# Feed-forward stage: the second products of a chunk's last two feature tiles as one block, token tile by token tile

## The chip, the core and the metric

The kernel runs on one core of a Trainium2 chip, as one program. The metric is the device time of one execution in microseconds (us). Before the change the median of three runs is 1665.53 us, the lowest 1661.75 and the highest 1668.51. Lower is better.

## What is computed

An attention with pooled queries (8 batches, 8 heads, 576 pooled query rows against 1152 keys, head size 64) is followed by a feed-forward part on its 4608 rows of 512 features. The change touches the feed-forward part alone:

```python
q_pool = q.reshape(B, H, S // factor, factor, D).mean(axis=3)
attn = softmax(scale * q_pool @ k^T);  x = (attn @ v), heads side by side   # 4608 x 512
h = x @ w_in            # 512 -> 2048
g = h - np.tanh(h)
out = g @ w_out         # 2048 -> 512
```

(The softmax line is the reference's five lines in short.)

## The kernel before

The attention fills the first half of the span and writes its result to `x_dram`; nothing of it changes. The feed-forward part then goes over the 4608 tokens in chunks: eight of 512 tokens and two of 256. Within a chunk it goes over 16 feature tiles of 128 hidden features, `fc` = 0 to 15 (`NF` = 16). Every fp32 operand is split into a high and a low part, so each product is three matmuls.

For one feature tile there are two blocks of work on TensorE (PE):

- the first product, in `hidden`: 12 matmuls into one buffer `ps_h` (three such PSUM buffers). We call it H(fc).
- the second product, in `second`: for each of the chunk's four token tiles of 128 tokens three matmuls that add `g_hi` and `g_lo` times `wo[fc]` into that token tile's sum. The sums lie in `ps_o`, four PSUM buffers, one for each token tile, and stay open over all 16 feature tiles. We call it S(fc): 12 matmuls.

Between the two, `hidden` makes g = h - tanh(h) from `ps_h`: six ScalarE (ACT) instructions (`g_u`, `g_t`, two `g_s`, `g_m` at lines 509 to 513, and `g_hi` at 520), six VectorE (DVE) ones (514 to 519) and `g_lo` on GpSimd (POOL). As this takes a while, a second product is made three feature tiles late: `waiting` holds what is still to be done, and after each H the oldest entry is taken once more than `LAG` = 3 are waiting (six in chunks of 256 tokens). A tick below marks the next chunk, so at a chunk's end PE's order is H15, S12, H0', S13, H1', S14, H2', S15, H3', S0'.

When S15 is done, `store` copies the four sums out of `ps_o` with four ACT instructions (line 539, into `o_s`, which has two buffers) and SP's queue sends each to `out`. S0' writes the same four `ps_o` buffers, so each token tile of S0' has to wait for its copy.

What sets the order: on PE, POOL and SP the instructions stand in the order of the code (`keep_in_program_order`). ACT and DVE are ordered by the tile framework's scheduler, which works from a timeline of its own at build time. Each engine then executes its list strictly in that order. The next chunk's rows of x are fetched by SP's queue at `fc` = 0, 3, 6 and 9 and divided and split on POOL up to `fc` = 12; `reciprocals` and the weight loads take place in the first chunk only.

The profile gives line 37 (the recording helper) to all PE, POOL and SP instructions; names of tiles tell them apart: `ps_h` is a first product, `ps_o` a second one, `o_s` a copy of a sum. `ps_o<-w` (a weight tile loaded ahead, `w`) marks S0 and S1, `ps_o<-wo` the others; `ps_h<-x,w` marks H0 to H3.

Of the kernel before, what the change touches and what calls it, by code (L numbers as in the profile page):

```python
# [8 lines left out]
F32 = mybir.dt.float32  # L9
# [34 lines left out]
def kernel(  # L44
# [18 lines left out]
    P = 128  # L63
    B, NP, _, _, SQ = q.shape
# [4 lines left out]
    DM, DFF = w_in.shape  # L69
    w_in, w_out = w_in.bitcast(I32), w_out.bitcast(I32)  # L70
    NF = DFF // P
# [22 lines left out]
    def load_x(tiles, raw, sp, mul, hi, t0, n):  # L94

        x_h, x_l = (t.rearrange("p (c n) -> p c n", c=NP) for t in tiles())

        t = {}

        def fetch(hp):  # L100
            x, r = t[hp] = raw(hp)
            sp.dma_start(x[:, 0:n], x_dram[hp, :, t0:t0 + n])
            c = t0
            while c < t0 + n:
                b, c1 = divmod(c, SQ)
                m = min(SQ - c1, t0 + n - c)
                for h in range(2):
                    sp.dma_start(r[h * 64:h * 64 + 64, c - t0:c - t0 + m],
                                 r_dram[b, hp, h:h + 1, c1:c1 + m].broadcast_to([64, m]))
                c += m  # L110

        def divide(hp):
            x, r = t[hp]
            mul.tensor_tensor(x[:, 0:n], x[:, 0:n], r[:, 0:n], op=ALU.mult)

        def hi_part(hp):
            hi(x_h[:, hp, 0:n], t[hp][0][:, 0:n])

        def lo_part(hp):
            mul.tensor_tensor(x_l[:, hp, 0:n], t[hp][0][:, 0:n], x_h[:, hp, 0:n].bitcast(F32), op=ALU.subtract)  # L120
        return x_h, x_l, [[lambda hp=hp, f=f: f(hp) for f in (fetch, divide, hi_part, lo_part)] for hp in range(NP)]
# [6 lines left out]
    def x_tile(i):  # L128
        return xp[i].tile([P, NP * 512], F32R, name="x")
# [5 lines left out]
    t, n = chunks.pop()  # L135
# [4 lines left out]
    with ExitStack() as actx:  # L140
# [10 lines left out]
        pe, act, dve, pool, sp = (InOrder(tc, e) for e in (nc.tensor, nc.scalar, nc.vector, nc.gpsimd, nc.sync))  # L151
# [185 lines left out]
        def reciprocals(eng, b, t):  # L337

            eng.tensor_scalar(t, t, 1e-9, None, op0=ALU.add)
            eng.reciprocal(t, t)  # L340

        def spread(dma, b, t):
            dma.dma_start(by_rows(r_dram[b]), t)
# [66 lines left out]
        wi, wo = [], []  # L410
# [39 lines left out]
        for u in range(end + 60):  # L450
            run(u, first)
            run(u, early)
            n, r = divmod(u, G)
# [19 lines left out]
    ps_o = ctx.enter_context(tc.tile_pool(name="ps_o", bufs=4, space=PSUM))  # L473

    pe, pool, sp = (InOrder(tc, e) for e in (nc.tensor, nc.gpsimd, nc.sync))
    halves = {}

    def weights(f1):
        while max(len(wi), len(wo)) < f1 or len(wo) < len(wi):
            f = len(wo)  # L480
            if f == len(wi):
                wi.append(wt.tile([P, 2, NP, P], F32R, name=f"wi{f}"))
                sp.dma_start(wi[f].bitcast(F32), wi_dram[f])
            if f >= len(wo):
                wo.append(wt.tile([P, 2, DM], F32R, name=f"wo{f}"))
                sp.dma_start(wo[f].bitcast(F32), wo_dram[f])
# [34 lines left out]
        pool.tensor_tensor(g_l, s1, g_h.bitcast(F32), op=ALU.subtract)  # L521
        return g_h, g_l, last

    def second(po, g_h, g_l, _, nt, fc):
        for j in range(nt):
            ts = slice(j * P, (j + 1) * P)
            for i, (g, w) in enumerate(((g_h, 0), (g_h, 1), (g_l, 0))):
                pe.matmul(po[j], g[:, ts], wo[fc][:, w],
                                 start=(fc == 0 and i == 0), stop=(fc == NF - 1 and i == 2))

    def store(po, t0, nt, ci):
        if ci == len(chunks) - 1:
            o_n = x_tile((ci + 1) % 2).bitcast(F32).rearrange("p (j n) -> p j n", n=DM)
        for j in range(nt):
            if ci == len(chunks) - 1:
                o_s = o_n[:, j]
            else:
                o_s = gp.tile([P, DM], F32, name="o_s", bufs=2)
            nc.scalar.activation(o_s, po[j], AF.Copy)  # L539
            sp.dma_start(out[t0 + j * P:t0 + (j + 1) * P, :], o_s)  # L540

    waiting = []
    xs = x0
    for ci, (t0, n) in enumerate(chunks):
        x_h, x_l, _ = xs
        po = []
        for fc in range(NF):
            if ci == 0:
                weights(min(NF, 5 + 2 * fc))

            load = []
            if ci + 1 < len(chunks):
                if fc == 0:
                    xs = load_x(lambda: (x_tile((ci + 1) % 2), x_tile((ci + 1) % 2)), x_raw, sp, pool,
                                lambda o, x: pool.tensor_scalar(o, x, 1.0, 0.0, op0=ALU.mult, op1=ALU.add), *chunks[ci + 1])
                load = [xs[2][(fc - x) // 3][i] for i, x in ((3, 3), (0, 0), (1, 2), (2, 2)) if (fc - x) % 3 == 0 and 0 <= fc - x < 3 * NP]
            for f in load:
                f()
            g = hidden(x_h, x_l, n, fc)
            if tot and fc == 3:  # L560
                with tc.issue_after(g[2]):
                    reciprocals(nc.vector, *tot[0])
                spread(sp, *tot.pop(0))

            def rest(po=po, g=g, fc=fc, t0=t0, nt=n // P, ci=ci):
                if fc == 0:
                    po += [ps_o.tile([P, DM], F32, name="ps_o") for _ in range(nt)]
                second(po, *g, nt, fc)
                if fc == NF - 1:
                    store(po, t0, nt, ci)  # L570
            waiting.append(rest)
            while len(waiting) > (LAG if n > 256 else 2 * LAG):
                waiting.pop(0)()
    while waiting:
        waiting.pop(0)()


_OUTS = [((4608, 512), 'float32')]
# [31 lines left out]
```

## Time and profile before

| | before |
|---|---|
| median of 3 runs, us | 1665.53 (1661.75 to 1668.51) |
| the profiled execution's own time, us | 1668.33 |
| its span, first to last instruction, us | 1666.5 |
| mean granted TensorE clock | 0.994 of full |
| PE busy in the span | 1621.7 us, 97% |
| DVE, ACT, POOL busy | 79%, 61%, 56% |

The feed-forward part takes the span from about 850 us to its end. In the profile a number in square brackets is idle time of the engine before an instruction, with what ended it. A row of the chain of waits is a piece of the path that ended last: its start, its length, and the work. A row of the view by stretches gives the stretch, its length, the busy time of PE with the count of its instructions, the granted clock (1.00 is full), the share of the DMA engines and GB/s.

### The profile page before, as it was taken

The numbers are of one execution on the slowest core, as the hardware profiler recorded it, in microseconds if no ns is written. First come the engines' busy times: TensorE is split into PE (matmuls) and PEld (weight loads), VectorE is DVE, ScalarE is ACT, GpSimd is POOL, SyncE is SP. The second block draws the span as 40 slices with busy tenths as digits, with TensorE's granted clock in tenths as the row PEclk, the third lists the DMA queues.
The fourth block names the chain that finished last, engine by engine and source line by source line (L and its number), as shares of the span: only waits on it lengthen the run. The fifth ranks groups of instructions, "written<-read, shape, count | busy, mean of one in ns | idle before, by whom it ended". The sixth has DMA issues, their size and how long they took to land.

```text
span 1666.5 us, 32223 instructions
## 1 busy us (share of the span) xinstructions
PE 1621.7 (97%) x12576; PEld 1251.9 (75%) x12576; DVE 1322.2 (79%) x1725; ACT 1021.2 (61%) x1865; POOL 939.8 (56%) x694
## 2 busy tenths in 40 slices
PE   5999999999999999999999999999999999999999
PEld 3666776777777677777778787887878787878897
DVE  7888889889888889888657677676767676776886
ACT  2655655656656556556566666566666666665776
POOL 2777878778778778778844243334334332422332
PEclk9999999999999999999999999999999999999999
DMA  3343443443344334335464101101010111010000
GB/s 139 118 136 107 139 136 108 126 134 122 124 128 130 124 115 144 123 106 163 143 242 158 38 26 40 37 14 51 26 51 26 38 39 38 26 37 15 25 27 26
DMA packets 72665, 147.86 MB, mean 89 GB/s; under 512 B 11136, under 2 KB 36672, under 8 KB 72512
## 3 DMA queue, kind: packets, MB, share of 16 engines
q1 hardware_dynamic: 72512, 145.80, 26.8%
q8 instruction: 99, 1.62, 0.4%
q14 instruction: 54, 0.44, 0.1%
HBM read 109.49 MB, written 36.27 MB: 87 GB/s over the span
## 4 chain that ended last, share of the span: by engine, by line
PE 84%; DVE 13%; ACT 2%; issue 1%; DMA 0%; DVEq 0%; ACTq 0%
PE ps L37 37%; PE ps_h L37 24%; PE ps_o L37 23%; DVE w L37 6%; DVE mx L37 6%; DVE nm L37 0%; DVE lo L37 0%; ACT g_s L512 0%; ACT g_m L513 0%; ACT g_s L511 0%; ACT g_u L509 0%; DMA q_n<-in_q_dram 0%; ACT g_hi L520 0%; ACT o_s L539 0%; ACT g_t L510 0%
## 5 line engine op out<-in xcount | busy, mean ns | idle before, releaser
L37 DVE TENSOR_REDUCE mx<-ps 128x2 f32<-128x768 f32 x480 | 434.3, 950 | 74.8 <-PE ps L37 74.7
L37 POOL TENSOR_TENSOR g_lo<-g_s,g_hi 128x512 fp32r<-128x512 f32 (+1 forms) x160 | 189.9, 1187 | 511.5 <-ACT g_hi L520 464.9
L37 ACT ACTIVATE p_f<-ps 128x576 f32<-128x576 f32 x576 | 361.5, 650 | 94.3 <-PE ps L37 79.7
L37 POOL TENSOR_TENSOR z<-p_f 128x576 f32<-128x576 f32 x192 | 279.6, 1456 | 154.7 <-ACT p_f L37 154.7
L37 PE MATMUL ps<-hi 64*128 64x288 f32 (+1 forms) x2112 | 316.9, 352 | 23.7 <-DVE mx L37 13.7
L37 PE MATMUL ps_h<-x,wi 128*128 128x512 f32 (+1 forms) x1440 | 327.2, 377 | 0.0
L37 PE MATMUL ps_o<-wo,g_hi 128*128 128x512 f32 x1008 | 311.6, 390 | 0.0
L37 PEld LDWEIGHTS ps_h<-x,wi 128*128 128x128 f32 x1440 | 260.0, 193 | 53.1
L37 PE MATMUL ps<-p_f,v 128*64 128x288 f32 x2304 | 293.5, 409 | 0.0
L37 PEld LDWEIGHTS ps<-hi 64*128 64x128 f32 x2112 | 194.6, 187 | 89.2 <-DVE mx L37 34.6
L509 ACT ACTIVATE g_u<-ps_h 128x512 f32<-128x512 f32 (+1 forms) x160 | 88.8, 555 | 267.8 <-PE ps_h L37 267.5
L37 PEld LDWEIGHTS ps<-p_f,v 128*64 128x64 f32 x2304 | 159.7, 137 | 113.7 <-ACT p_f L37 12.0
L514 DVE SCALAR_TENSOR_TENSOR ps_w<-g_u,ps_h 128x512 f32<-128x512 f32 (+1 forms) x160 | 102.9, 643 | 178.7 <-ACT g_t L510 177.0
L37 PEld LDWEIGHTS ps_o<-wo,g_hi 128*128 128x128 f32 x1008 | 187.5, 188 | 39.1
L37 POOL TENSOR_TENSOR z<-z,p_f 128x576 f32<-128x576 f32 x128 | 194.0, 1516 | 11.9 <-ACT p_f L37 2.0
L37 PE MATMUL ps_o<-wo,g_lo 128*128 128x512 f32 x504 | 196.3, 389 | 0.0
L37 PE MATMUL ps<-lo,hi 64*128 64x288 f32 x1152 | 171.0, 293 | 0.0
L37 PE MATMUL ps<-hi,lo 64*128 64x288 f32 x1152 | 170.9, 293 | 0.0
L37 PE MATMUL ps<-mb,ones_k 64*128 64x288 f32 x1152 | 170.3, 292 | 0.0
L37 ACT ACTIVATE o_s<-ps 128x288 f32<-128x288 f32 x64 | 26.3, 411 | 230.3 <-PE ps L37 230.3
L519 DVE COPY_PREDICATED g_s<-g_m,g_t 128x512 f32<-128x512 int32 (+1 forms) x160 | 116.2, 726 | 17.1 <-DVE g_s L518 0.9
L517 DVE SCALAR_TENSOR_TENSOR ps_w<-g_s,ps_w 128x512 f32<-128x512 f32 (+1 forms) x160 | 102.9, 643 | 16.6 <-ACT g_m L513 0.5
(68 smaller groups left out, 2398.9 us busy)
## 6 DMA issues: line engine op xcount, KB each, us to landing
q_n<-in_q_dram SPq DMA_DIRECT2D x32, 576.0 KB
kq<-in_k_dram SPq DMA_DIRECT2D x32, 576.0 KB
v<-in_v_dram SPq DMA_DIRECT2D x32, 576.0 KB
x_dram<-o_s SPq DMA_DIRECT2D x32, 288.0 KB
out_dram<-o_s SPq DMA_DIRECT2D x34, 256.0 KB
w_raw<-in_moe_w_in_dram SPq DMA_DIRECT2D x16, 512.0 KB
wi_dram<-w_hl SPq DMA_DIRECT2D x16, 512.0 KB
w_raw<-in_moe_w_out_dram SPq DMA_DIRECT2D x16, 512.0 KB
```

The costliest lines, as they stand in the source:

```text
L37: ins = self.tc.keep_in_program_order(f(*args, **kwargs))
L509: nc.scalar.activation(u, h, AF.Square)
L514: nc.vector.scalar_tensor_tensor(w, u, -P0, h, op0=ALU.add, op1=ALU.mult)
L517: nc.vector.scalar_tensor_tensor(w, s2, P2, w, op0=ALU.add, op1=ALU.mult)
L519: last = nc.vector.copy_predicated(s1, m.bitcast(I32), th).ins
```

## The change

`rest` is no longer a closure that makes one S; it takes an entry from `waiting`, and when that entry is feature tile 14 (`NF - 2`) it takes the one for 15 as well and makes both: for each token tile the three matmuls of 14 and then the three of 15. `store` follows at once. Nothing is added or left out; the same matmuls, copies and transfers are issued.

```diff
-    def second(po, g_h, g_l, _, nt, fc):
+    def second(po, j, g_h, g_l, fc):
+        ts = slice(j * P, (j + 1) * P)
+        for i, (g, w) in enumerate(((g_h, 0), (g_h, 1), (g_l, 0))):
+            pe.matmul(po[j], g[:, ts], wo[fc][:, w], start=(fc == 0 and i == 0), stop=(fc == NF - 1 and i == 2))
+
+    def rest():
+        po, nt, t0, ci, *x = waiting.pop(0)
+        x = [x]
+        if x[0][-1] == 0:
+            po += [ps_o.tile([P, DM], F32, name="ps_o") for _ in range(nt)]
+        if x[0][-1] == NF - 2:
+            x.append(waiting.pop(0)[4:])
         for j in range(nt):
-            ts = slice(j * P, (j + 1) * P)
-            for i, (g, w) in enumerate(((g_h, 0), (g_h, 1), (g_l, 0))):
-                pe.matmul(po[j], g[:, ts], wo[fc][:, w],
-                                 start=(fc == 0 and i == 0), stop=(fc == NF - 1 and i == 2))
+            for g in x:
+                second(po, j, *g)
+        if len(x) == 2:
+            store(po, t0, nt, ci)
...
-            def rest(po=po, g=g, fc=fc, t0=t0, nt=n // P, ci=ci):
-                if fc == 0:
-                    po += [ps_o.tile([P, DM], F32, name="ps_o") for _ in range(nt)]
-                second(po, *g, nt, fc)
-                if fc == NF - 1:
-                    store(po, t0, nt, ci)
-            waiting.append(rest)
+            waiting.append((po, n // P, t0, ci, *g[:2], fc))
             while len(waiting) > (LAG if n > 256 else 2 * LAG):
-                waiting.pop(0)()
+                rest()
     while waiting:
-        waiting.pop(0)()
+        rest()
```

On PE, at the first chunk's end, the order before is: the end of S14, then H2' (`ps_h_13198`), then S15 (`wo15`) over its four token tiles (`ps_o_12484` to `ps_o_12487`).

```order
L37 MATMUL ps_o_12487<-wo14_12560,g_lo_13023 128x512
L37 MATMUL ps_h_13198<-x_12302,w02_126 128x512 x4
L37 MATMUL ps_h_13198<-x_12303,w02_126 128x512 x4
L37 MATMUL ps_h_13198<-x_12302,w02_126 128x512 x4
L37 MATMUL ps_o_12484<-wo15_12612,g_hi_13068 128x512 x2
L37 MATMUL ps_o_12484<-wo15_12612,g_lo_13069 128x512
L37 MATMUL ps_o_12485<-wo15_12612,g_hi_13068 128x512 x2
L37 MATMUL ps_o_12485<-wo15_12612,g_lo_13069 128x512
L37 MATMUL ps_o_12486<-wo15_12612,g_hi_13068 128x512 x2
L37 MATMUL ps_o_12486<-wo15_12612,g_lo_13069 128x512
L37 MATMUL ps_o_12487<-wo15_12612,g_hi_13068 128x512 x2
L37 MATMUL ps_o_12487<-wo15_12612,g_lo_13069 128x512
```

In the order after, S14 (`wo14`) and S15 alternate by token tile ahead of H2' (here `ps_h_13222`). These rows are the last token tile of that block, then H2', H3' (`ps_h_13264`) and the start of S0' (`w03`).

```order
L37 MATMUL ps_o_12487<-wo14_12560,g_hi_13022 128x512 x2
L37 MATMUL ps_o_12487<-wo14_12560,g_lo_13023 128x512
L37 MATMUL ps_o_12487<-wo15_12612,g_hi_13068 128x512 x2
L37 MATMUL ps_o_12487<-wo15_12612,g_lo_13069 128x512
L37 MATMUL ps_h_13222<-x_12302,w02_126 128x512 x4
L37 MATMUL ps_h_13222<-x_12303,w02_126 128x512 x4
L37 MATMUL ps_h_13222<-x_12302,w02_126 128x512 x4
L37 MATMUL ps_h_13264<-x_12302,w04_128 128x512 x4
L37 MATMUL ps_h_13264<-x_12303,w04_128 128x512 x4
L37 MATMUL ps_h_13264<-x_12302,w04_128 128x512 x4
L37 MATMUL ps_o_13298<-w03_127,g_hi_13123 128x512 x2
L37 MATMUL ps_o_13298<-w03_127,g_lo_13124 128x512
```

So PE's order becomes H15, S12, H0', S13, H1', then S14 and S15 together, H2', H3', S0': S15 has moved ahead of H2', and two first products now stand between the last matmul of a sum and S0'.

On ACT at the same place, the order before has the second and third copy, then six instructions on H3' (`ps_h_13264`) and H2' (`g_hi_13217`), and the fourth copy behind them.

```order
L539 ACTIVATE o_s_13247<-ps_o_12485 128x512
L539 ACTIVATE o_s_13250<-ps_o_12486 128x512
L509 ACTIVATE g_u_13277<-ps_h_13264 128x512
L510 ACTIVATE g_t_13278<-ps_h_13264 128x512
L520 ACTIVATE g_hi_13217<-g_s1_13213 128x512
L511 ACTIVATE g_s2_13280<-g_u_13277,pc_65 128x512
L512 ACTIVATE g_s1_13279<-g_u_13277,pc_65 128x512
L513 ACTIVATE g_m_13281<-g_u_13277,pc_65 128x512
L539 ACTIVATE o_s_13253<-ps_o_12487 128x512
```

In the order after, the copies (now line 552) stand behind the last instruction of H1' (`g_m_13167`), with the `g_hi` of H1' (`g_hi_13169`) in their middle, and ahead of all of H2' (`ps_h_13222`).

```order
L513 ACTIVATE g_m_13167<-g_u_13163,pc_65 128x512
L552 ACTIVATE o_s_13208<-ps_o_12484 128x512
L552 ACTIVATE o_s_13211<-ps_o_12485 128x512
L520 ACTIVATE g_hi_13169<-g_s1_13165 128x512
L552 ACTIVATE o_s_13214<-ps_o_12486 128x512
L552 ACTIVATE o_s_13217<-ps_o_12487 128x512
L509 ACTIVATE g_u_13235<-ps_h_13222 128x512
```

The four copies have moved ahead of the six instructions of H2' and the six of H3'. DVE, POOL and SP keep their orders.

## The prediction

> **What bounds the kernel now.** I read the page first. PE is busy for 97% of the span, and the chain of work that ended last runs through PE:
>
> ```profile
> PE 1621.7 (97%) x12576; PEld 1251.9 (75%) x12576; DVE 1322.2 (79%) x1725; ACT 1021.2 (61%) x1865; POOL 939.8 (56%) x694
> PE 84%; DVE 13%; ACT 2%; issue 1%; DMA 0%; DVEq 0%; ACTq 0%
> ```
>
> The change leaves the number of matmuls as it is, so it can only win where PE stands still or runs slowly. The waits of the feed-forward part (from 870 us on) say where PE stands still there: for one thing only, the copies out of `ps_o`. PE is named with the idle time after the modelled end of its last matmul, PEld with that of the weight load ahead of it:
>
> ```profile
> PEld ps_o L37 <- ACT o_s L539: 16.4, 7, 2.3
> PE ps_o L37 <- ACT o_s L539: 13.3, 7, 1.9
> ```
>
> Seven waits: one for each of the seven boundaries between two chunks of 512 tokens. The chain of waits shows one of them in order of time. It goes through H3', then through the whole ACT list behind it up to the fourth copy, and back to PE; after that H4' takes 4.34 us where others take 2.80 or less:
>
> ```profile
> 1032.83 2.75 PE ps_h L37 x12
> 1035.57 0.02 issue
> 1035.59 0.60 ACT g_u L509
> 1036.19 0.48 ACT g_t L510
> 1036.68 0.52 ACT g_hi L520
> 1037.20 0.61 ACT g_s L511
> 1037.81 0.61 ACT g_s L512
> 1038.42 0.61 ACT g_m L513
> 1039.03 0.49 ACT o_s L539
> 1039.52 0.04 issue
> 1039.57 0.97 PE ps_o L37 x3
> 1040.53 4.34 PE ps_h L37 x12
> ```
>
> The last view is the one by stretches, for the clock. The first pair below is the first boundary, the second pair the last of the six that look like it; the last two rows hold the wait of the fourth boundary:
>
> ```profile
> 945.25:948.66 3.41, 1.50 (x7) 1.00 0.11 42
> 948.66:952.07 3.41, 3.41 (x9) 0.50 0.60 179
> ...
> 1494.79:1498.20 3.41, 1.51 (x7) 1.00 0.11 41
> 1498.20:1501.62 3.42, 3.42 (x10) 0.50 0.35 113
> ...
> 1218.31:1221.72 3.41, 2.77 (x12) 1.00 0.41 154
> 1221.72:1225.14 3.42, 2.15 (x9) 1.00 0.35 99
> ```
>
> In six of the seven boundaries a stretch of 3.41 us in which PE was busy for only 1.50 is followed by one of the same length at half clock. In the fourth the wait fell across the edge of two such stretches (0.64 us of it in the one, 1.27 in the other), and the clock stayed full. So each wait costs its own length, and six of them a slow stretch after it.
>
> **What one boundary costs, and what the change gives back.** The price of the wait is taken from the fourth boundary, where the clock is not mixed in: S0' from its first matmul to the next block, against S1' of the same form two blocks later.
>
> ```profile
> 1218.82:1223.80 4.98, 3.07 (x14) 1.00 0.28 104
> 1226.76:1229.56 2.80, 2.80 (x13) 1.00 0.09 30
> ```
>
> 4.98 - 2.80 = 2.18 us: the 1.91 us of idle and the refilling of the pipeline. Seven of them are 15.3 us. From below, the idle time alone is 13.3 us, and from above the weight loads' 16.4. The price of the slow stretch is H4' in the chain, 4.34 us, against the same H4' in the fourth boundary, which the chain gives so:
>
> ```profile
> 1223.96 2.80 PE ps_h L37 x12
> ```
>
> 4.34 - 2.80 = 1.54 us, six times 9.2 us. (Where the slow stretch began earlier, part of it falls into S0', but it is as long.) From above, 3.41 us at half clock lose at most 1.71 us, six times 10.2. Together 15.3 + 9.2 = 24.5 us, between 22.5 and 26.6.
>
> The Trainium skill speaks against the second half of this: its page "TensorE: Matmul & The Clock Gate", section "HAM oscillation — how this bites in real kernels", lets TensorE stand idle for up to some 3.4 us before its clock falls. By that rule waits of 1.91 us cost no clock, and the sum would be 15.3 us alone. The trace does not agree: six such waits have a stretch at 0.50 behind them. I take the trace.
>
> The change removes this if the four copies are done when S0' is due. I follow the second boundary in the timeline: S14 starts at 1024.41, H2' at 1027.17, S15 at 1029.90, S0' at 1035.39, with H3' between the last two. The rows are those that the steps below rest on (start, length, instruction):
>
> ```profile
> 1020.85 1.30 POOL L37 TENSOR_TENSOR g_lo<-g_s,g_hi 128x512 fp32r<-128x512 f32 x1 [4.21 <-ACT g_hi L520]
> 1024.41 0.62 PE L37 MATMUL ps_o<-wo,g_hi 128*128 128x512 f32 x2
> 1025.10 0.62 PE L37 MATMUL ps_o<-wo,g_hi 128*128 128x512 f32 x2
> 1027.17 2.89 PE L37 MATMUL ps_h<-x,w 128*128 128x512 f32 x12
> 1027.33 0.72 ACT L513 ACTIVATE g_m<-g_u,pc 128x512 f32<-128x512 f32 x1
> 1029.32 0.75 DVE L519 COPY_PREDICATED g_s<-g_m,g_t 128x512 f32<-128x512 int32 x1
> 1029.90 0.62 PE L37 MATMUL ps_o<-wo,g_hi 128*128 128x512 f32 x2
> 1031.22 0.70 DVE L514 SCALAR_TENSOR_TENSOR ps_w<-g_u,ps_h 128x512 f32<-128x512 f32 x1 [1.15 <-ACT g_t L510]
> 1031.59 0.60 ACT L539 ACTIVATE o_s<-ps_o 128x512 f32<-128x512 f32 x1
> 1035.39 0.63 PE L37 MATMUL ps_o<-w,g_hi 128*128 128x512 f32 x2
> 1037.28 1.28 POOL L37 TENSOR_TENSOR g_lo<-g_s,g_hi 128x512 fp32r<-128x512 f32 x1 [2.18 <-ACT g_hi L520]
> ```
>
> In the new order S14 and S15 fill 1024.41 to 1029.90 (two blocks, 2.76 and 2.73), H2' takes 1029.90 to 1032.65, H3' the same place as before, and S0' is due at 1035.39 again. On ACT `g_m` of H1' ends at 1028.05, and by then the first two sums are done (a sum takes 5.49 / 4 = 1.37 us, so they end at 1025.8 and 1027.2). Two copies of 0.5 to 0.6 us end near 1029.1. `g_hi` of H1' waits for line 519, 1029.32 + 0.75 = 1030.07, and ends near 1030.7; the other two copies end near 1031.9, the last sum having been done at 1029.9. That is 3.5 us ahead of S0', so PE does not stop. ACT's next work, `g_u` of H2', only comes at 1032.65, so the copies delay nothing.
>
> What is moved, and what hides it:
>
> - S15 is due earlier, at its first matmul 0.69 us into the joint block (1025.10) in place of 1029.90. It needs `g_lo` of feature tile 15, which the first row shows to end at 1022.15. 2.95 us are left, and this is the next thing to be late.
> - H2' comes 2.73 us later, and H3' follows without a gap, so DVE starts feature tile 2' at about 1034.0 and then has two waiting. It has room: in the 512-token part it idles 157.2 us ahead of line 514 in 122 feature tiles, 1.29 us each, so some three tiles take up the delay.
>
> ```profile
> L514 DVE SCALAR_TENSOR_TENSOR ps_w<-g_u,ps_h 128x512 f32<-128x512 f32 x122 | 85.0, 696 | 157.2 <-ACT g_t L510 157.2
> ```
>
> - Who waits for that is S2', four blocks behind S0', near 1046.4. Line 514 of 2' to its `g_lo` takes 1031.22 to 1038.56 now, 7.34 us, so 2' is there by 1041.4, and 5 us are left. H5' and H6', which use the same `ps_h` buffers again, are due later than the reading of them by several us too.
> - The four stores on SP's queue keep their place ahead of the next fetch of x and go out earlier; that fetch waits less. The third copy takes the first one's `o_s` buffer again 2.7 us after the first began (1028.0 to 1030.7); should the first store not have landed by then, ACT waits. The trace has such a wait once, 0.2 us, and 3.5 us would hide it.
>
> ```profile
> ACT o_s L539 <- DMA out_dram<-o_s: 0.2, 1, 0.2
> ```
>
> - Two S, and then two H, without the other kind between them: the nearest row is the end of the kernel, where seven S of 256 tokens stand in a row. They take 9.56 / 42 = 0.228 us for a matmul, S14 above 2.76 / 12 = 0.230. I take 0, and 0.1 us either way for each boundary, under 1 us in all.
>
> ```profile
> 1653.11 9.56 PE ps_o L37 x42
> ```
>
> At the very end the second copy still follows PE's last matmul: 0. The boundaries into and between the 256-token chunks have no wait now, and stay so: 0.
>
> The profiled execution would go from a span of 1666.5 to 1642.0 us. Its own time, 1668.33, lies 0.2% above the median, so the sum is taken off the median: 1665.53 - 24.5 = **1641.0 us**. A measurement of this kernel tells about 0.5%, 8.3 us, from no change: its own three runs span 0.4%.
>
> **The rivals.**
>
> *The slow stretches stay.* If half clock came not from the wait but from something else at a boundary, such as the burst of transfers (a DMA share of 0.60 in the slow stretch), only the waits would go: 1665.5 - 15.3 = 1650.2. Against it speaks the fourth boundary, which has the transfers at 0.35 to 0.41 and no slow stretch, and the equal length and grid of the stretches. The rule of the Trainium skill named above would lead to this result. Chance 0.06.
>
> *Nothing is won.* PE's wait is hidden time for DVE; were DVE the real limit, PE would stop a few feature tiles later for as long, in front of S2' or H6', and the time would stay at 1665.5. The 1.29 us of DVE idle per feature tile speak against it. Chance 0.04.
>
> *Slower: PE waits for S15's operands.* The joint block needs `g_lo` of tile 15 at 1025.10. If it came later than now by more than 2.95 us, for instance because POOL or ACT is held up, PE would stop there at each boundary, with all of H2', H3' and S0' behind it. As late as S15's old start, the wait is 4.8 us, and with refilling (0.27) and a slow stretch (1.54) seven of them are 46 us against the 24.5 saved: 1687 us. It turns into a loss from a wait of about 1.7 us on (1.7 + 0.27 + 1.54 = 24.5 / 7). ACT's, DVE's and POOL's lists are unchanged up to the joint block, so I see no cause. Chance 0.03.
>
> **How the numbers follow.** The forecast has the remaining 0.87. Its own range is 22.5 to 26.6 us saved, 1 us either way for the blocks, and the spread of the runs, 3.8 us down and 3.0 up: 1634 to 1647. That leaves out all three rivals, 0.13, and a little of the forecast, so it is also the range. Faster by over 0.5% (below 1657.2) holds for the forecast and the first rival: 0.93. Within 0.5%: 0.04. Slower: 0.03.
>
> **What would show it.** The waits of PE in the feed-forward part for `o_s` should be gone or under 1 us in all, and no other wait of PE should take their place. The granted clock should be full at all boundaries, with no H of 4.34 us. The rows of ACT should have the fourth copy done some 3.5 us ahead of S0', and DVE idle about 4 us at each boundary ahead of 2' and then little for about three tiles. `g_lo` of tile 15 should still end about 3 us before S15. A PE wait on `g_lo` in the joint block, half clock without a wait, or a new wait in front of S2' would prove the forecast wrong.

## The result, and the profile after

| | before | after |
|---|---|---|
| median of five runs, us | 1665.53 (1661.75 to 1668.51) | 1643.30 (1642.87 to 1646.48) |
| the profiled execution's own time, us | 1668.33 | 1643.04 |
| its span, us | 1666.5 | 1641.3 |
| PE busy in the span, us | 1621.7 | 1609.8 |

The ratio of the runs is 0.9864 (0.9851 to 0.9876): 22.2 us less by the medians. The spans of the two profiled executions differ by 25.2 us.

The first and the fourth part of the page after, the same two lines as before: PE is busy for 11.9 us less with the same 12576 matmuls, and ACT's share of the chain that ended last has gone from 2% to 0%. Most of the 11.9 us is the work that no longer runs at half clock (6 x 1.54 = 9.2); another 1.9 is the seven S0' blocks that held a wait, busy for 3.07 us each where a block without one is busy for 2.80.

```profile
PE 1609.8 (98%) x12576; PEld 1245.2 (76%) x12576; DVE 1319.6 (80%) x1725; ACT 1023.9 (62%) x1865; POOL 942.9 (57%) x694
PE 85%; DVE 13%; issue 1%; ACT 0%; DMA 0%; DVEq 0%; ACTq 0%
```

These are all the waits of the feed-forward part after, from 860 us on (total, times, longest). No row of PE or of its weight loads (PEld) is left; before there were 13.3 and 16.4 us for `o_s`.

```profile
POOL g_lo L37 <- ACT g_hi L520: 429.6, 139, 5.7
ACT g_u L509 <- PE ps_h L37: 232.7, 135, 2.2
DVE ps_w L514 <- ACT g_t L510: 138.7, 107, 3.9
POOL g_lo L37 <- issue: 38.1, 15, 3.6
ACT g_hi L520 <- DVE g_s L519: 18.8, 26, 1.8
POOL x_f L37 <- DMA x_r<-r_dram: 8.9, 2, 5.1
ACT x L552 <- PE ps_o L37: 5.1, 2, 4.3
ACT g_s L512 <- POOL g_lo L37: 1.2, 4, 0.4
DVE g_s L519 <- DVE g_s L518: 0.9, 2, 0.5
DVE ps_w L517 <- DVE ps_w L516: 0.5, 1, 0.5
DVE g_s L518 <- ACT o_s L552: 0.5, 1, 0.5
ACT o_s L552 <- DMA out_dram<-o_s: 0.4, 1, 0.4
```

The chain of waits after, at the second boundary: H1', the joint block of 24 matmuls, H2' and H3' in one row, S0', H4'. Nothing but PE is on it, and each row has the length of its matmuls at full pace. H4' takes 2.80 us where it took 4.34. In the whole trace after no stretch between 40 and 1640 us is at half clock.

```profile
1017.71 2.73 PE ps_h L37 x12
1020.45 5.48 PE ps_o L37 x24
1025.93 5.45 PE ps_h L37 x24
1031.38 2.80 PE ps_o L37 x12
1034.18 2.80 PE ps_h L37 x12
```

The timeline after at the same place. `g_lo` of feature tile 15 ends at 1016.73 + 1.30 = 1018.03, and S15 begins at 1020.97. The copies run in two pairs, the last one ending at 1027.84, with S0' at 1031.22. DVE stands idle for 3.87 us ahead of feature tile 2', then has no wait ahead of 3' (the row at 1034.06) and 4'.

```profile
1016.73 1.30 POOL L37 TENSOR_TENSOR g_lo<-g_s,g_hi 128x512 fp32r<-128x512 f32 x1 [4.20 <-ACT g_hi L520]
1020.97 0.62 PE L37 MATMUL ps_o<-wo,g_hi 128*128 128x512 f32 x2
1023.82 1.08 ACT L552 ACTIVATE o_s<-ps_o 128x512 f32<-128x512 f32 x2
1026.57 1.27 ACT L552 ACTIVATE o_s<-ps_o 128x512 f32<-128x512 f32 x2
1029.82 0.69 DVE L514 SCALAR_TENSOR_TENSOR ps_w<-g_u,ps_h 128x512 f32<-128x512 f32 x1 [3.87 <-ACT g_t L510]
1031.22 0.63 PE L37 MATMUL ps_o<-w,g_hi 128*128 128x512 f32 x2
1034.06 0.71 DVE L514 SCALAR_TENSOR_TENSOR ps_w<-g_u,ps_h 128x512 f32<-128x512 f32 x1
```

Where the 25.2 us came from is read from the chains of both traces: the rows of H0' of the third, fourth and fifth boundary, first before, then after.

```profile
1108.63 2.75 PE ps_h L37 x12
...
1199.77 2.73 PE ps_h L37 x12
...
1290.50 2.75 PE ps_h L37 x12
```

```profile
1100.74 2.75 PE ps_h L37 x12
...
1188.09 2.73 PE ps_h L37 x12
...
1276.61 2.75 PE ps_h L37 x12
```

From the third to the fourth H0', a stretch that holds a wait with a slow stretch behind it, the time went from 91.14 to 87.35 us: 3.79 saved. From the fourth to the fifth, with a wait alone, from 90.73 to 88.52: 2.21 saved. Measured in the same way from one S0' to the next, all six of the former kind saved 3.72 to 3.84 us and the one of the latter 2.15, together 24.8. The rest lies ahead of the first boundary, where the change does nothing: the first chunk's S0' happened to start at 860.95 us in place of 861.31.

### The profile page after: what moved, and what is told of

It is laid out like the page before. It is cut to its first block, busy times and chain, and to the rows that moved or that the text cites. A ratio compares the mean times of both kernels' runs of the same rounds, so it can differ in the third digit from the quotient of the medians.

```text
span 1641.3 us, 32231 instructions
## 1 busy us (share of the span) xinstructions
PE 1609.8 (98%) x12576; PEld 1245.2 (76%) x12576; DVE 1319.6 (80%) x1725; ACT 1023.9 (62%) x1865; POOL 942.9 (57%) x694
## 4 chain that ended last, share of the span: by engine, by line
PE 85%; DVE 13%; issue 1%; ACT 0%; DMA 0%; DVEq 0%; ACTq 0%
PE ps L37 37%; PE ps_h L37 24%; PE ps_o L37 24%; DVE w L37 6%; DVE mx L37 6%; DVE nm L37 0%; DVE lo L37 0%; DMA q_n<-in_q_dram 0%; ACT hi L37 0%; DVE rec L37 0%; DVE kq L37 0%; ACT p_f L37 0%; DVEq L37 0%; ACT x L552 0%; ACT z_s L37 0%
## 5 line engine op out<-in xcount | busy, mean ns | idle before, releaser
L37 PE MATMUL ps_h<-x,wi 128*128 128x512 f32 (+1 forms) x1440 | 318.3, 370 | 0.0
L37 PEld LDWEIGHTS ps_h<-x,wi 128*128 128x128 f32 x1440 | 253.1, 188 | 50.5
```

The source lines that it names most:

```text
L37: ins = self.tc.keep_in_program_order(f(*args, **kwargs))
```

## The experiments

**Theory A** is that of the prediction: PE's wait for the fourth copy, and the half clock that follows it, are all that is won, and only the time at which that copy is done counts. The rivals are in the expectations. Ratios are to the kernel before on the same chip, with 95% intervals. No kernel here leaves out work of the reference; three of them add matmuls whose results nobody reads.

### S15 early, but not alternating (e1_move_only)

```diff
-        for j in range(nt):
-            for g in x:
+        for g in x:
+            for j in range(nt):
                 second(po, j, *g)
```

> The changed kernel, but S14 is made whole and then S15 whole (no alternation by token tile), at the same place behind H1'. Theory A (the gain is PE's wait for the fourth copy and the half clock behind it, and only the time at which that copy is done counts): the last sum is done at the same time, so all copies are done about 3.5 us ahead of S0', no PE wait for o_s, no half clock, ratio to before 0.986, about 1643 us. Rival B (the alternation matters, since it gives the copies their sums one by one): the copies crowd behind S15 and part of the wait comes back, ratio 0.990 to 0.997.

Measured: 1643.70 us (1643.14 to 1645.35), ratio 0.9858 (0.9843 to 0.9872). There is no PE wait in the feed-forward part, and the copies come only 0.1 us later than in the changed kernel, measured from the block's start (1020.70 here, 1020.28 there), as the timeline shows (two rows of two copies; H2' here begins at 1026.18, S0' at 1031.64):

```profile
1024.35 1.28 ACT L552 ACTIVATE o_s<-ps_o 128x512 f32<-128x512 f32 x2
1027.11 1.28 ACT L552 ACTIVATE o_s<-ps_o 128x512 f32<-128x512 f32 x2
1031.64 0.63 PE L37 MATMUL ps_o<-w,g_hi 128*128 128x512 f32 x2
```

So the alternation is not needed when S15 is early. Rival B falls.

### Alternating, but not early (e2_join_only)

```diff
-            while len(waiting) > (LAG if n > 256 else 2 * LAG):
+            while len(waiting) > (LAG if n > 256 else 2 * LAG) + (waiting[0][-1] == NF - 2):
                 rest()
```

> S14 and S15 made together by token tile, but at S15's old place behind H2', so the sums are done no earlier than before. Theory A: the alternation alone lets the first copies start early, the fourth (whose sum is done some 2.7 us ahead of S0') is placed ahead of H3' on ACT and is done before S0' needs it; no PE wait, ratio 0.986 to 0.988, about 1643 to 1646 us. Rival C (the gain needs S15 early, two first products between it and S0'): the wait of about 1.9 us stays at seven boundaries, ratio 0.997 to 1.000.

Measured: 1643.31 us (1642.77 to 1643.81), ratio 0.9854 (0.9837 to 0.9870), again without a PE wait. Each half of the change alone does the whole, so S15 need not be early either. The waits show what it leans on here: ACT's copies wait for an earlier store to have left its buffer, nine times and for up to 1.1 us, and PE's slack hides it. The second row is such a fourth copy; it is done at 1030.58, ahead of the `g_u` of H3', and PE comes to the fourth token tile of S0' at 1033.62.

```profile
ACT o_s L552 <- DMA out_dram<-o_s: 7.5, 9, 1.1
...
1029.98 0.60 ACT L552 ACTIVATE o_s<-ps_o 128x512 f32<-128x512 f32 x1 [0.96 <-DMA out_dram<-o_s]
```

### PE's order as before, four copy buffers (e3_more_os)

```diff
-                o_s = gp.tile([P, DM], F32, name="o_s", bufs=2)
+                o_s = gp.tile([P, DM], F32, name="o_s", bufs=4)
```

> The kernel before with four o_s buffers for the copies in place of two; PE's order is untouched. Theory A: the fourth copy no longer has to wait for the second one's store, is done right behind the third and about 2 us ahead of need; no PE wait for o_s and no half clock at the boundaries, ratio 0.986 to 0.988, about 1643 to 1646 us. Rival C (PE's order is the cause): nothing changes, 1665 us.

Measured: 1644.72 us (1643.27 to 1645.77), ratio 0.9862 (0.9847 to 0.9876). With PE's order of the kernel before, the last three copies stand one behind the other ahead of `g_u` of H3', and are done at 1032.15; S0' begins at 1032.05 and comes to its fourth token tile at 1034.16.

```profile
1028.25 0.60 ACT L539 ACTIVATE o_s<-ps_o 128x512 f32<-128x512 f32 x1
...
1030.57 1.58 ACT L539 ACTIVATE o_s<-ps_o 128x512 f32<-128x512 f32 x3
1032.25 0.60 ACT L509 ACTIVATE g_u<-ps_h 128x512 f32<-128x512 f32 x1
```

So the two buffers are part of the cause. The fourth copy takes the second one's buffer and may not start before that one's store has landed; with two buffers the scheduler put six instructions on H3' and H2' ahead of it, with four buffers it did not. (That its build-time timeline had the store land late is the likely reason; no run shows it.) On the chip both the list and the store count. In the trace before, ACT comes to the fourth copy without idle time, at 1038.92, so there its place in the list held it. But the second copy's store had landed only at 1037.49, which is about when PE was due at the fourth token tile (1035.39 and three groups of 0.70 us). Listed first, the fourth copy would still have ended near 1038.1 (an estimate: 1037.49 + 0.59), and some 0.6 of the 1.91 us of idle would have stayed. PE's order was one way around this, two more buffers are another. Rival C falls.

### The wait filled with work (e4_fill)

```diff
...
+            if nt == 4 and j == 3 and fc == 0 and t0 > 0:
+                h = ps_h.tile([P, 512], F32, name="ps_h")
+                for i in range(9):
+                    pe.matmul(h, g_h[:, 0:P], wo[fc][:, 0], start=True, stop=True)
...
```

(The two other lines of the edit hand `t0` to `second`.)

> The kernel before with nine useless matmuls of 512 columns into a free ps_h buffer, put ahead of the fourth token tile of S0' at the seven boundaries, where PE waits; the wait itself is not shortened. Theory A (the half clock comes from PE standing idle): PE is busy through the wait, H4' takes 2.7 to 2.8 us at every boundary, no stretch at 0.50, and the 9.2 us of slow stretches are won: 1655 to 1658 us, ratio 0.994 to 0.995. Rival D (the half clock comes from something else at the boundary, such as the burst of transfers for x): six stretches at half clock stay, 1665 us or a little more, ratio 1.000.

Measured: 1659.84 us (1658.46 to 1660.89), ratio 0.9952 (0.9937 to 0.9967), span 1656.7: the ratio is as expected, and the median lies 2 us above the range given. The view by stretches has S0' with the nine matmuls in it at 4.98 us, as long as it was with the wait, all of it busy; the H4' behind it takes 2.80 at full clock, while the transfers are as dense as ever (a DMA share of 0.72):

```profile
1033.47:1038.45 4.98, 4.98 (x22) 3.87 (x21) 3.39 (x6) 3.93 (x7) 2.56 (x2) 1.00 0.29 107
1038.45:1041.25 2.80, 2.80 (x13) 2.26 (x12) 0.95 (x2) 0.63 (x1) 1.01 (x1) 1.00 0.72 216
```

(Its columns from the third on: busy time of PE, PEld, DVE, ACT and POOL, clock, DMA share, GB/s.) No stretch at half clock is left at any boundary. So the half clock comes from PE standing idle, not from the transfers; rival D falls. The two parts of the gain can now be told apart by spans: 1666.5 - 1656.7 = 9.8 us for the slow stretches (of which 0.3 lie ahead of the first boundary), 1656.7 - 1641.3 = 15.4 us for the seven waits, 2.2 us each.

### How early S15 may come (e5 to e8)

Four kernels bring S15 further ahead, to find where its operands are late. In e5 the joint block stands behind S13; in the others S13 joins it, with 2, 3 or 4 groups of three matmuls ahead of the first S15 group. The first diff below is that of e5, the second that of e6, with its list cut short; e7 and e8 differ from e6 in the order of the first entries of `EARLY`.

```diff
-            while len(waiting) > (LAG if n > 256 else 2 * LAG):
+            while len(waiting) > (LAG if n > 256 else 2 * LAG) - (waiting[0][-1] == NF - 2 and n > 256):
                 rest()
```

```diff
...
+EARLY = [(13, 0), (14, 0), (15, 0), (13, 1), (14, 1), (15, 1), ...]
...
+        if x[0][-1] == NF - 3 and nt == 4 and len(waiting) > 2:
+            x += [waiting.pop(0)[4:], waiting.pop(0)[4:]]
+            for f, j in EARLY:
+                second(po, j, *x[f - 13])
+            return store(po, t0, nt, ci)
```

> The changed kernel with the joint block of S14 and S15 one H earlier, right behind S13, so that H1', H2' and H3' follow each other. Theory A with the prediction's account of what is late next (g_lo of tile 15): S15 is due 2.7 us earlier than in the changed kernel, of 2.95 us; its g_lo matmul, the third of the three, has some 0.6 us left. No PE wait, no half clock, 1643 to 1645 us, ratio 0.985 to 0.987. Rival E (DVE, given three feature tiles at once, has less room than its idle time says): PE waits ahead of H5', H6' or S2' for DVE, 1 to 3 us at each boundary, 1650 us or more.

> S13, S14 and S15 together by token tile at S13's place behind H0' (the third rival of the prediction on purpose: PE comes to S15 before its operands are there). S15's first matmul is due 1.38 us behind the block's start and its first g_lo matmul 1.84 us; in the changed kernel's trace g_hi of tile 15 is there about 1.85 us and g_lo 3.25 us behind that start. Theory A: PE waits about 1.4 us in all at each of seven boundaries, 7 x (1.4 + 0.27) = 11.7 us, and half clock comes back behind some or all of them, up to 7 x 1.55 = 10.9: 1655 to 1666 us. If a wait at this place costs nothing (some other slack takes it up): 1643 us.

> As the kernel before this one, with one group of three matmuls more ahead of the first S15 group (S13 and S14 of token tile 0, S13 of tile 1). Theory A: g_lo is due 0.69 us later, so PE waits about 0.7 us at each boundary, 7 x (0.7 + 0.27) = 7 us: 1650 us if waits of 0.7 us leave the clock full, up to 1661 if they do not. This tells how short a wait may be before half clock follows.

> As the one before, with one more group ahead of the first S15 group (S13 and S14 of token tiles 0 and 1). Theory A: g_lo is due when it is there, the wait is between 0 and 0.1 us at each boundary, and the time is that of the changed kernel within 2 us, 1643 to 1646 us.

| kernel | S15 earlier than in the changed kernel by, us | time, us | ratio | span, us |
|---|---|---|---|---|
| e5_joint_at_h0 | 2.7 | 1643.56 | 0.9871 (0.9856 to 0.9887) | 1640.9 |
| e8_early_4 | 3.4 | 1644.82 | 0.9880 (0.9865 to 0.9896) | 1642.6 |
| e7_early_3 | 4.1 | 1649.56 | 0.9905 (0.9889 to 0.9922) | 1648.1 |
| e6_early_2 | 4.8 | 1654.15 | 0.9934 (0.9919 to 0.9949) | 1652.2 |

The waits of e6 and of e7 (total, times, longest; line 40 is the recording helper there):

```profile
PEld ps_o L40 <- POOL g_lo L40: 7.8, 7, 1.1
PEld ps_o L40 <- ACT g_hi L523: 5.2, 7, 0.8
...
PE ps_o L40 <- POOL g_lo L40: 4.8, 7, 0.7
PE ps_o L40 <- ACT g_hi L523: 2.3, 7, 0.3
```

```profile
PEld ps_o L40 <- POOL g_lo L40: 7.2, 7, 1.0
...
PE ps_o L40 <- POOL g_lo L40: 4.1, 7, 0.6
```

By the spans, a place 2.7 us earlier costs nothing, 3.4 us earlier 0.2 us for each boundary (1642.6 - 1641.3 over seven), and from there on each further step of 0.7 us costs 0.6 to 0.8. e6 came out a little faster than expected (1655 to 1666): PE idles 1.0 us at a boundary there and not 1.4, and no clock is lost. The operands of tile 15 are what is late next, as the prediction said, and there is a little more room than it said: the first matmuls of a group need `g_hi` alone, and only the third needs `g_lo`. e5 also has three H in a row with no PE wait behind them, so rival E falls: DVE has the room for three feature tiles at once. In e6 and e7 no slow stretch follows the waits, though PE idles 1.0 and 0.6 us at each boundary.

### How short a wait leaves the clock alone (e9, e10)

The filled kernel with one and with two useless matmuls in the wait (`range(1)`, `range(2)` in place of `range(9)`).

> The kernel before with one useless matmul in PE's wait at each boundary in place of the nine of the filled one, so that PE idles about 1.7 us at a boundary in place of 1.91. If half clock follows once PE is busy for less than half of a 3.41 us stretch, it is busy for about 1.73 (51%) here and the clock stays full or falls at a boundary or two only: 1656 to 1660 us. If a gap of 1.3 us or more is enough, six or so stretches at half clock stay: 1664 to 1667 us.

> The same with two useless matmuls, idle about 1.45 us at a boundary. Half-busy rule: busy for about 1.96 of 3.41 us (57%), the clock stays full, 1655 to 1659 us. If gaps of 1.3 us or more are enough: half clock at about six boundaries, 1664 to 1667 us.

Measured: 1658.86 us (1658.50 to 1659.17), ratio 0.9956 (0.9940 to 0.9972), with one; 1659.13 (1658.56 to 1660.86), 0.9961 (0.9945 to 0.9977), with two (a shade above its range of 1655 to 1659). PE's waits in the one with one matmul (its mean granted clock is 1.000):

```profile
PEld ps_o L37 <- ACT o_s L543: 14.8, 7, 2.1
PE ps_o L37 <- ACT o_s L543: 11.7, 7, 1.7
```

The seven waits are almost all there, 1.68 us each in place of 1.91, and yet no stretch at half clock is left: one matmul in each wait is worth the whole 9.4 us (span 1666.5 to 1657.1). This is not because the waits happened to fall across two stretches: four of the seven lie wholly in one, like the one in the first row here, and the stretch behind it keeps the full clock.

```profile
945.05:948.46 3.41, 1.73 (x9) 1.00 0.17 64
948.46:951.87 3.41, 3.41 (x15) 1.00 0.55 174
```

With 1.91 us of idle in one stretch, PE is busy for 1.50 of 3.41 us, 44%; with 1.68, for 1.73, 51%.

## Why the prediction was right

- **The waits.** Forecast 7 x 2.18 = 15.3 us, measured 15.4 (e4 against the changed kernel) and 2.21 at the boundary that had a wait alone. The price was right because it was read from whole blocks, 4.98 against 2.80; the sum of PE's idle time, 13.3, would have been 2 us short, and that of PEld's, 16.4, a little too much.
- **The slow stretches.** Forecast 6 x 1.54 = 9.2 us, measured 9.4 to 9.8 by spans (e9, e4). That they come from the waits was argued from the one boundary whose wait had no slow stretch behind it; e4, e9 and e10 show it. The rule of the Trainium skill's page "TensorE: Matmul & The Clock Gate", section "HAM oscillation — how this bites in real kernels", that gaps up to some 3.4 us do no harm, does not hold here: 1.91 us within one stretch was enough in six of six cases, and 1.68 us within one stretch was not in four of four.
- **The sum.** 24.5 us against 25.2 by the profiled spans and 22.2 by the medians. The term that is too large for the medians is that of the slow stretches: it was taken from the profiled execution, which at 1668.33 us is one of the slower of its kind, and taken off the median. e9, which wins back the slow stretches alone, gains 9.4 us by the profiled spans but 6.7 by the medians (1665.53 to 1658.86), about four slow stretches' worth and not six's; the waits are worth 15.6 by the medians (1658.86 to 1643.30, though on two chips). Whether a wait falls into one stretch or across two would depend on when the execution starts, so that not every run has six; this is argued, not shown, as only the profiled executions have traces. The runs that list their clock do not settle it: the 23 of the kernel before have spans of 1660.5 to 1668.5 us at 0.990 to 0.996 of full, but the clock does not put the spans in order (1663.1 and 1666.7 both at 0.994), and the changed kernel too has a run of 1644.7 at 0.997 beside its 1641.3 at 0.999.
- **The cover.** The copies were done 3.4 us ahead of S0' (forecast 3.5), `g_lo` of tile 15 was there 2.94 us ahead of S15 (2.95), DVE idled 3.87 us ahead of 2' (about 4). No wait of PE took the old one's place.
- **What the prediction missed** is the reason for the fourth copy's late place: it said that the copy is behind six instructions of H3', and not that the two `o_s` buffers had a part in that. The change's two halves, which it counted as one, each do the whole (e1, e2), and so do two more buffers with PE's order untouched (e3).

## What to carry to other kernels

When an engine that is busy for 97% waits for the same thing at every boundary of a loop, price the wait by the whole block against the same block without it, and look at the clock behind it: here a third of the loss was not idle time at all. Then ask why the awaited instruction stands where it does in its engine's list; too few buffers for what it writes can put it there, and more buffers are a smaller edit than another order of the work (here two more; one more was not tried). Before work is moved earlier, find the operand that is late next and how far away it is; here that was some 3 us, and a place 2.7 us earlier cost nothing.

## What the runs showed of the hardware that was not expected

- In these traces the clock goes by how busy TensorE was in a stretch of 3.41 us on a fixed grid (the first and the last slow stretch before begin at 948.66 and 1498.20 us, 161 such lengths apart). After a stretch with 1.50 us busy the next one ran at 0.50, six times of six; after one with 1.73 (e9, four times) or 2.15 (the fourth boundary before) it stayed at 1.00. So the limit lies between 44% and 51%. Each of these stretches held one piece of idle time, so a limit on the busy time and one on the longest idle piece within a stretch are not told apart. Nine useless matmuls in each wait, or one, kept the clock full.
- A wait cost PE more than its idle time in the three kernels where this can be read: 2.2 us for 1.91 of idle (before), 0.97 for 0.59 (e7), 1.56 for 1.0 in two pieces (e6). The idle time of the weight loads, 2.3, 1.0 and 1.9 us, was more than the cost each time.
